# Fp32 gated attention mix: weights' loads and roundings, first keys, clearing, turned maxima, gate and last loads in other places

## The chip, the cores and the metric

The kernel runs on one core of a Trainium2 chip. The metric is device microseconds of one execution, as the median of several runs. Engines: PE is TensorE (matrix products), DVE is VectorE, ACT is ScalarE, POOL is GpSimd, SP is SyncE, which here issues nearly all DMAs. SP's queue is worked in order, so a DMA that waits for something holds up those behind it.

## The reference, cut to what matters

```python
# S=2048 tokens, D=448, H=16 heads of 28; x is A_x for both branches
g = sigmoid((x * gate_w).sum(-1, keepdims=True))
# A: each query sees 8 keys, at offsets 0, 2, ... 14 behind it
q, k, v = split_heads(x @ A_wqkv)
a = softmax(einsum("bhsd,bhswd->bhsw", q, k[idx]) * 28**-0.5, masked) @ v[idx]   # then merged @ A_wo
# B: full attention, 16 heads, 2048 x 2048 scores each
q, k, v = split_heads(x @ B_wqkv)
b = softmax(einsum("bhqd,bhkd->bhqk", q, k) * 28**-0.5) @ v                       # then merged @ B_wo
return g * a + (1 - g) * b
```

## The kernel before

Every fp32 product is computed as three products of rounded parts: an operand is split into a high part (`hi`, `xh`, `wh`: a ScalarE copy that rounds to fp32r) and a low part (`lo`, `xl`, `wl`: a subtraction, on VectorE or POOL), and high·high, high·low and low·high are summed in PSUM. Rounding a weight set thus costs ScalarE copies and POOL subtractions (`split_w`, in four pieces of its rows) once its load (`load_w`, tiles `raw` and, for the last 64 rows, `wt`) has landed.

The instructions of every engine run in the order in which the program writes them; no scheduler moves them. Order is therefore set by the loops and by small tables in the text.

**Projections.** A loop over 92 tiles `n`, in this order: tiles 0 to 11 (first queries and keys of B, weight set 0), 12 to 23 (set 1) and 24 to 27 (set 2), 512 tokens by 128 columns each; 28 to 43 values of B (set 3), 44 to 59, 60 to 75 and 76 to 91 the queries, keys and values of A (sets 4, 5, 6), each 128 tokens by 448 columns. From tile 10 on a tile is accumulated in two halves in two PSUM banks: ScalarE evacuates both (`raw`, L336 and L350), POOL adds them (L338, L351). For a q/k tile a step `finish` one tile later rounds (`qkh`, L341), and POOL subtracts (L342); both parts are stored to DRAM (`qk_hi`, `qk_lo`) and loaded again as keys (`KH`) and queries (`QP`). For A's tiles POOL adds into a staging tile `ast`, stored to `a_scr` every second tile. The last two columns of set 4 carry the gate (`zt`).

From tile 11 on TensorE works score products (L141, `s1`) into the projections, four per tile, of which VectorE takes maxima (`MX`, L158) for the softmax of B. When a group of 512 queries is through, `max_parts` splits its maxima, `max_turn` transposes them on VectorE (`nms`, L182) and `max_store` puts them in DRAM, the last two one tile later.

The table `loads` tells at which tile each weight set's load is written, `splits` at which two tiles its rounding is, two pieces per tile. After the exponential of the gate (n = 64) come a transposition of `1-g` on TensorE (n = 65), a copy `omT`, a store and sixteen loads `og`, then the first queries of the main stage (n = 66). SBUF tiles come from rings: the evacuations `raw` from a pool `pp` of eight (`pair`), weights and `ast` from a ring of three.

**Main stage.** 16 units (4 groups of heads by 4 blocks of 512 queries) of 16 key steps: step `st = 16u + kt` makes four score tiles on TensorE, two exponentials on ScalarE (`P`, L998) and the value products `av` of the step before (L957). Branch A (softmax over 8 taps) runs on POOL, VectorE and DMA beside it. `at(kind, st, f)` writes `f` into a step, at its start ("pre"), between the score tiles ("mid") or at its end. When A is done, `a_done(st)` loads the output weights and rounds one of seven blocks a step (`split_wo`). At a unit's end `fin_copy` copies its result out of PSUM (`osb`, L813) and an epilogue of seven more steps divides and stores it (`on_hi`, `on_lo`).

**Output products.** In the last 20 steps (from st = 236) TensorE also works the output projection for 16 tiles `j` of 128 rows. `op_queue(j)` lists its items: `op_mm` for seven blocks of rows (A's in `oah`, `oalo`, B's in `onhi`, `onlo`), `op_t` and `op_split` (transpose and split A's result of tile `j+1`, loaded into `oal` by `op_load_a`), `op_out`. `op_some(st, 7)` takes seven items a step; an item whose number in `READY` is above `st` stops the queue. `op_load_b(b, k)` loads B's results. After the last step come the leftovers, `op_rest` (the last head block of tiles 8 to 11), the last epilogue (`fin_t`, `fin_rec`, ...) and tiles 12 to 15.

Of the kernel before, what the change touches and what calls it, by code (L numbers as in the profile page):

```python
# [25 lines left out]
def gated_mix_kernel(ctx: ExitStack, tc: tile.TileContext, xT, xn, gw, wA, wB, woAB, out):  # L26
# [74 lines left out]
    def load_k(g, t, src):  # L101
        for h in range(4):
            r = D + 112 * g + DH * h
            dma_r(t[32 * h:32 * h + DH, :], src[r:r + DH, :])
# [85 lines left out]
    init_kh(KH[0])  # L190
# [6 lines left out]
    with tc.tile_pool(name="xp", bufs=1) as xp, tc.tile_pool(name="wp", bufs=2) as wp:  # L197
# [3 lines left out]
        def raw3():  # L201
            return wp.tile([128, 3, 450], F32, tag="raw", name="raw", bufs=3)
# [34 lines left out]
        def load_w(wi, tails=(False, True)):  # L237
            src, cols = WSRC[wi]
            if wi not in wraw:
                wraw[wi] = raw3(), ptile("wt"), sum(c1 - c0 for c0, c1 in cols) + 2 * (wi == GATE)  # L240
            r, t, _ = wraw[wi]
            for tail in tails:
                o = 0
                for c0, c1 in cols:
                    e = o + c1 - c0
                    if tail:
                        both(t[:, o:e], src[384:448, c0:c1])
                    else:
# [109 lines left out]
        def a_tile(n, i, j):  # L358
            k = j // 8
            if j % 2 == 0:  # L360
                stage[k] = wp.tile([128, 3, 450], F32, tag="raw", name="ast", bufs=3).rearrange(
                    "p a b -> p (a b)")[:, 0:896].rearrange("p (c j e) -> p c j e", c=8, j=2)
            add_halves(n, stage[k][:, :, j % 2, :], zt[:, j:j + 1] if tiles[n][0] == GATE else None)
            if j % 2 == 1:
                nc.sync.dma_start(a_own[i][:, :, j - 1:j + 1, :].rearrange("c p j e -> p c j e"), stage[k])
# [29 lines left out]
        nc.scalar.activation(zt, zt, AF.Exp)  # L395
        nc.scalar.activation(wh0[:, 0:3, wa], wr0, AF.Copy)
# [38 lines left out]
        firsts = [min(n for n, t in enumerate(tiles) if t[0] == wi) for wi in range(len(WSRC))]  # L435

        loads = {2: 17, 3: 22, **{wi: firsts[wi - 1] for wi in (4, 5, 6)}}
        splits = {1: firsts[1] - 4, 2: firsts[2] - 4, 3: firsts[3] - 4, **{wi: firsts[wi - 1] + 2 for wi in (4, 5, 6)}}
        for n, t in enumerate(tiles):
# [4 lines left out]
            for w in splits:  # L444
                if splits[w] <= n < splits[w] + 2:
                    split_w(w, (2 * (n - splits[w]), 2 * (n - splits[w]) + 1))
# [18 lines left out]
            if n == 4:  # L465
                for t in (*QP[0], *QP[1]):
                    nc.gpsimd.memset(t.bitcast(F32), 0.0)
            if n == 7:
                load_k(0, KH[0], qk_hi)
                load_qhi(0)  # L470
            if n == 8:
                for i in (1, 2):
                    nc.sync.dma_start(a_scr[i][:, 0:NJ, :].rearrange("c j e -> c (j e)").rearrange(
                        "c (a b) -> c a b", b=NJ), omg[0:8, None, :].to_broadcast([8, 56, NJ]))
            if n == 9:
                init_kh(KH[1])
                nc.gpsimd.memset(V[:, :, :, DH:], 1.0)
# [4 lines left out]
            if parts:  # L482
                u, t = parts.pop(0)
                max_store(u, max_turn(t))
            if finished and n < len(tiles) - 2:
                u = finished.pop(0)
                parts.append((u, max_parts(u)))
# [6 lines left out]
            if n == 65:  # L494
# [9 lines left out]
            if n == 66:  # L504
                load_q(0)
# [239 lines left out]
    def a_done(st):  # L745
        adone.append(st)
        load_wo()
        for k in range(7):
            at("pre", st + k + 1, lambda k=k: raw_wo(k))
            at("act", st + 6 + k, lambda k=k: split_wo(k))  # L750
# [174 lines left out]
    def op_queue(j):  # L925
# [7 lines left out]
            (0, lambda: op_split(j + 1)),  # L933
            (0, lambda: op_mm(j, bank, (2,))),
# [10 lines left out]
    READY[1, 3] = OP0 + 22  # L945
    for k in range(4):
        at("end", OP0 + 7 + k, lambda k=k: op_load_b(0, k))
        at("end", OP0 + 13 + k if k < 3 else OP0 + 18, lambda k=k: op_load_b(1, k))
# [56 lines left out]
    def op_some(st, n):  # L1005
        while n:
            if not opq:
# [4 lines left out]
                if j % 4 == 0 and 4 <= j:  # L1012
                    b = j // 4 + 1
                    for k in range(3):
                        op_load_b(b, k)
# [6 lines left out]
    for u in range(NU):  # L1022
        g, b = divmod(u, NB)
        for kt in range(NJ):
# [40 lines left out]
            if not OPS and s1c[0] == s1e:  # L1065
                s1_close()
                at("pre", st + 1, lambda: op_t(0))
                at("mid", st + 1, lambda: op_split(0))
# [10 lines left out]
    op_rest(9, accs[1])  # L1079
    fin_t(15)  # L1080
    fin_rec(15)
    op_rest(10, order[2])
    op_rest(11, order[3])
# [47 lines left out]
```

## Time and profile before

Three runs took 950.68, 952.6 and 953.49 us, median 952.6. The profiled execution took 950.85 us, its span is 949.1 us, and 1.75 us lie outside it. The mean granted clock of TensorE is 0.99.

| stage | us from the span's start | TensorE |
|---|---|---|
| projections, full tiles 0 to 9 | to about 34 | products |
| projections, half tiles with score products | about 34 to 277 | products, with the waits below |
| main stage without output products | 277 to 818 | two exponentials of about 1.0 us a step on ScalarE set the pace, 2.3 us |
| output products in the steps | 818 to 919 | 2.9 to 5.8 us a step |
| after the last `av` | 919 to 949 | products |

Rows read like this: start, duration, engine, line, instruction, result and operands; in brackets the idle time before it on its engine and what ended that. The pace of the projections is seen in evacuations two tiles apart, 5.81 us for q/k tiles and 5.25 us for A's:

```profile
70.19 1.03 ACT L336 ACTIVATE raw<-r 128x1024 f32<-128x1024 f32 x1 [1.48 <-PE r L284]
76.00 1.03 ACT L336 ACTIVATE raw<-r 128x1024 f32<-128x1024 f32 x1 [1.07 <-PE r L284]
...
224.49 0.92 ACT L350 ACTIVATE raw<-r 128x896 f32<-128x896 f32 x1 [1.62 <-PE r L289]
229.74 0.92 ACT L350 ACTIVATE raw<-r 128x896 f32<-128x896 f32 x1 [1.62 <-PE r L289]
```

### The profile page before, as it was taken

How to read it: one execution, taken by the hardware profiler on the slowest of the kernel's cores; microseconds unless marked ns; L12 is line 12 of the kernel's file. 1: busy time of each engine (PE TensorE's matmuls, PEld its weight loads, DVE VectorE, ACT ScalarE, POOL GpSimd, SP SyncE). 2: the span in 40 equal slices, each digit the busy share in tenths (PEclk: the TensorE clock that was granted, in tenths of full speed). 3: DMA queues.
4: the chain of work that ended last, by engine and by line, in shares of the span. 5: the costliest groups of instructions: out<-in, count | busy, mean ns of one | idle time of the engine just before them, and what ended most of it. 6: DMA issues, size and time to landing. Idle time of an engine off the chain costs nothing.

```text
span 949.1 us, 21412 instructions
## 1 busy us (share of the span) xinstructions
PE 921.4 (97%) x8398; PEld 548.4 (58%) x8398; DVE 735.9 (78%) x979; ACT 649.5 (68%) x798; POOL 621.4 (65%) x487
## 2 busy tenths in 40 slices
PE   8899899989999999999999999999999999999998
PEld 6798799979974444444444444444444443465657
DVE  6387699989978999999999999999998888400012
ACT  4355434333358888888888888888988889755541
POOL 2388746554448899999999999999993943100000
PEclk9999899999999999999999999999999999999999
DMA  9847403364437242333335331531412133344332
GB/s 277 249 169 218 151 1 89 84 162 117 111 106 225 71 130 55 84 98 89 91 89 127 108 92 45 133 97 25 106 42 52 32 77 105 112 143 128 108 111 87
DMA packets 101054, 104.36 MB, mean 110 GB/s; under 512 B 61676, under 2 KB 71292, under 8 KB 100056
## 3 DMA queue, kind: packets, MB, share of 16 engines
q1 hardware_dynamic: 100808, 102.72, 38.5%
q8 instruction: 66, 1.08, 0.5%
q10 hardware_dynamic: 144, 0.26, 0.1%
q14 instruction: 36, 0.29, 0.1%
HBM read 61.99 MB, written 40.48 MB: 108 GB/s over the span
## 4 chain that ended last, share of the span: by engine, by line
PE 87%; DMA 4%; POOL 3%; ACT 2%; SPq 2%; issue 2%; DVE 1%; ACTq 0%; POOLq 0%; DVEq 0%
PE T L995 29%; PE av L957 25%; PE r L289 13%; PE T L797 7%; PE r L284 4%; PE T L141 4%; PE r L141 3%; POOL qkh L342 1%; ACT P L998 1%; PE T L775 1%; POOL raw L338 1%; DMA wt<-in_wA 1%; DMA V<-in_xT 1%; SPq L98 1%; POOL wl L206 1%
## 5 line engine op out<-in xcount | busy, mean ns | idle before, releaser
L998 ACT ACTIVATE P<-T 128x1024 f32<-128x1024 f32 x512 | 497.2, 1024 | 96.6 <-PE T L995 95.9
L145 DVE TENSOR_REDUCE MX<-T 128x1 f32<-128x512 f32 x470 | 443.4, 954 | 42.0 <-PE T L141 17.2
L957 PE MATMUL av<-P,V 128*32 128x512 f32 x2048 | 272.7, 605 | 0.4 <-ACT osb L813 0.4
L995 PEld LDWEIGHTS T<-QH,KH 30*128 30x128 f32 x1024 | 91.2, 181 | 234.2 <-ACT P L998 203.2
L995 PE MATMUL T<-QH,KH 30*128 30x512 f32 x1024 | 221.3, 491 | 4.7 <-ACT P L998 3.3
L158 DVE TENSOR_REDUCE MX<-r 128x2 f32<-128x1024 f32 x160 | 192.2, 1221 | 38.2 <-PE r L141 37.1
L141 PE MATMUL T<-KH,QP 28*128 28x512 f32 x704 | 221.4, 460 | 0.0
L995 PE MATMUL T<-QH,KL 28*128 28x512 f32 x1024 | 189.2, 394 | 0.0
L995 PE MATMUL T<-QL,KH 28*128 28x512 f32 x1024 | 187.7, 393 | 0.0
L595 POOL TENSOR_TENSOR prod<-qt,kt 128x896 f32<-128x896 f32 x64 | 135.1, 2115 | 7.7 <-DMA kt<-a_scr 7.7
L350 ACT ACTIVATE raw<-r 128x896 f32<-128x896 f32 (+1 forms) x64 | 58.8, 919 | 99.4 <-PE r L289 95.6
L650 POOL TENSOR_TENSOR oat<-oat,prod 128x896 f32<-128x896 f32 x56 | 118.0, 2107 | 2.4
L141 PEld LDWEIGHTS T<-KH,QP 28*128 28x128 f32 x704 | 86.0, 181 | 23.2 <-ACT P L998 13.3
L645 POOL TENSOR_TENSOR prod<-vt,L 128x896 f32<-128x896 f32 x56 | 95.3, 1702 | 0.6
L141 PE MATMUL r<-KH,QP 64*128 64x512 f32 x320 | 90.6, 397 | 3.8 <-DMA QP<-qk_hi 2.6
L351 POOL TENSOR_TENSOR ast<-raw 128x448 f32<-128x448 f32 x48 | 55.1, 1151 | 59.1 <-ACT raw L350 37.2
L995 PEld LDWEIGHTS T<-QL,KH 28*128 28x128 f32 x1024 | 92.7, 184 | 0.0
L995 PEld LDWEIGHTS T<-QH,KL 28*128 28x128 f32 x1024 | 92.1, 183 | 1.0
L289 PE MATMUL r<-wh,xh 64*128 64x448 f32 (+1 forms) x512 | 84.7, 368 | 5.2 <-ACT raw L350 4.9
L957 PEld LDWEIGHTS av<-P,V 128*32 128x32 f32 x2048 | 40.3, 108 | 79.5 <-issue 73.8
L785 DVE TENSOR_TENSOR oalo<-T,oah 128x384 fp32r<-128x384 f32 x16 | 8.9, 557 | 88.3 <-ACT onhi L784 80.1
L289 PE MATMUL r<-wh,xl 64*128 64x448 f32 (+1 forms) x384 | 70.1, 366 | 0.0
(111 smaller groups left out, 1144.4 us busy)
## 6 DMA issues: line engine op xcount, KB each, us to landing
a_scr<-ast SPq DMA_DIRECT2D x24, 448.0 KB
qk_hi<-qkh SPq DMA_DIRECT2D x24, 256.0 KB
qk_lo<-qkh SPq DMA_DIRECT2D x24, 256.0 KB
rbc<-rs SPq DMA_DIRECT2D x60, 64.0 KB
KH<-qk_hi SPq DMA_DIRECT2D x16, 224.0 KB
QP<-qk_hi SPq DMA_DIRECT2D x64, 56.0 KB
KL<-qk_lo SPq DMA_DIRECT2D x16, 224.0 KB
QH<-qk_hi SPq DMA_DIRECT2D x64, 56.0 KB
```

The source lines that it names most:

```text
L141: nc.tensor.matmul(bank, qhis[u][h % 2][r, 128 * qs:128 * qs + 128], KH[u // NB % 3][r, 512 * kc:512 * kc + 512], start=True, stop=True)
L145: nc.vector.tensor_reduce(MX[:, n % NMX:n % NMX + k], bank, axis=X, op=ALU.max)
L158: nc.vector.tensor_reduce(m, PM[k], axis=X, op=ALU.max)
L289: nc.tensor.matmul(bank[:, 0:cols], x, ws[c][rows, k, 0:cols], start=first, stop=last)
L350: nc.scalar.activation(raw[:, :, 0:cols], PJ[n % 2][:, :, 0:cols], AF.Copy)
L595: nc.gpsimd.tensor_tensor(out=p, in0=qt[c], in1=kvt["k", c % 2][:, HALO - DIL * w:HALO - DIL * w + NJ, :], op=ALU.mult)
L645: nc.gpsimd.tensor_tensor(out=dst.rearrange("p j (h d) -> p j h d", d=DH), in0=kvt["v", c % 2][:, HALO - DIL * w:HALO - DIL * w + NJ, :].r ...
L650: nc.gpsimd.tensor_tensor(out=oat[c], in0=oat[c], in1=oat[c, w], op=ALU.add)
L797: writes(bank, nc.tensor.matmul(bank[:, :D], src, wo[c][:, k, :], start=(first and k == ks[0] and i == 0), stop=(last and k == ks[-1] and ...
L957: nc.tensor.matmul(av[32 * h:32 * h + 32, :], V[:, kt, 4 * g + h, :], tiles_[h], start=(kt == 0), stop=(kt == NJ - 1), skip_group_check=True)
L995: nc.tensor.matmul(bank[a], (KH[g % 3], KH[g % 3], KL[g % 2])[t][r, ks], (qh, ql, qh)[t][r, :], start=(t == 0), stop=(t == 2))
L998: nc.scalar.activation(p, RP[0] if a == "2" else mine, AF.Exp, scale=SCALE)
```

## The change

It gives other places to things that are done in any case; the mathematics is the same, and no product is added or removed. Line numbers of the changed kernel are up to five higher.

- First keys: the first queries are loaded at tile 3 (they were at 7), the first keys in two pieces, columns 0 to 1536 at tile 7 and the rest at tile 8.
- Weights: sets 2 to 6 are loaded at tiles 12, 16, 26, 40, 56 (before 17, 22, 28, 44, 60); set 3 is rounded at 24 and 25 as before, sets 4, 5 and 6 in four tiles each from 34, 48, 64 (before two tiles from 30, 46, 62). `wt` has a ring of its own, the weights' ring has two buffers, and `ast` comes from the ring of eight.
- Clearing: four `QP` buffers on ScalarE at the start (POOL at tile 4), `KH[1]` at the start (tile 9), ones into `V` at tile 32 (tile 9), the two small stores of zeros at 16 (8).
- Maxima are turned and stored three tiles after they are split (one before); gate transposition and first queries of the main stage at 68 and 69 (65 and 66).
- Last part: output weights' roundings three steps later (`d`; in this program `a_done` falls at 217, which gives 3), first `op_split` at the step's end, `op_load_b` as an item behind `op_split` for tiles 4 and 8, the last block of b = 1 loaded at OP0+16 and used from OP0+18 (OP0+18, OP0+22), `op_rest` in another order around the last epilogue's transposition.

```diff
-    init_kh(KH[0])
+    for t in KH:
+        init_kh(t)
...
-            return wp.tile([128, 3, 450], F32, tag="raw", name="raw", bufs=3)
+            return wp.tile([128, 3, 450], F32, tag="raw", name="raw", bufs=2)
...
-                wraw[wi] = raw3(), ptile("wt"), sum(c1 - c0 for c0, c1 in cols) + 2 * (wi == GATE)
+                wraw[wi] = raw3(), wp.tile([128, 450], F32, tag="wt", name="wt"), sum(c1 - c0 for c0, c1 in cols) + 2 * (wi == GATE)
...
-                stage[k] = wp.tile([128, 3, 450], F32, tag="raw", name="ast", bufs=3).rearrange(
-                    "p a b -> p (a b)")[:, 0:896].rearrange("p (c j e) -> p c j e", c=8, j=2)
+                stage[k] = pair("ast").rearrange("p a b -> p (a b)")[:, 0:896].rearrange("p (c j e) -> p c j e", c=8, j=2)
...
+        for t in (*QP[0], *QP[1]):
+            nc.scalar.activation(t, t0, AF.Copy)
         nc.scalar.activation(wh0[:, 0:3, wa], wr0, AF.Copy)
...
-        loads = {2: 17, 3: 22, **{wi: firsts[wi - 1] for wi in (4, 5, 6)}}
-        splits = {1: firsts[1] - 4, 2: firsts[2] - 4, 3: firsts[3] - 4, **{wi: firsts[wi - 1] + 2 for wi in (4, 5, 6)}}
+        loads = {2: 12, 3: 16, 4: 26, 5: 40, 6: 56}
+        splits = {1: (8, 2), 2: (20, 2), 3: (24, 2), 4: (34, 1), 5: (48, 1), 6: (64, 1)}
...
-            if n == 4:
-                for t in (*QP[0], *QP[1]):
-                    nc.gpsimd.memset(t.bitcast(F32), 0.0)
+            if n == 3:
+                load_qhi(0)
             if n == 7:
-                load_k(0, KH[0], qk_hi)
-                load_qhi(0)
+                load_k(0, KH[0], qk_hi, slice(0, 1536))
             if n == 8:
+                load_k(0, KH[0], qk_hi, slice(1536, S))
+            if n == 16:
                 for i in (1, 2):
                     nc.sync.dma_start(a_scr[i][:, 0:NJ, :].rearrange("c j e -> c (j e)").rearrange(
                        "c (a b) -> c a b", b=NJ), omg[0:8, None, :].to_broadcast([8, 56, NJ]))
-            if n == 9:
-                init_kh(KH[1])
+            if n == 32:
                 nc.gpsimd.memset(V[:, :, :, DH:], 1.0)
...
-            if parts:
-                u, t = parts.pop(0)
+            if parts and parts[0][0] <= n:
+                _, u, t = parts.pop(0)
                 max_store(u, max_turn(t))
-            if finished and n < len(tiles) - 2:
+            if finished and n < len(tiles) - 3:
                 u = finished.pop(0)
-                parts.append((u, max_parts(u)))
+                parts.append((n + 3, u, max_parts(u)))
...
-            if n == 65:
+            if n == 68:
                 b = PJ[(n + 1) % 2][:, 0, :]
                 nc.tensor.transpose(b[0:NJ, 0:128], omg, ident)
...
-            if n == 66:
+            if n == 69:
                 load_q(0)
...
+        d = -(st + 6) % NJ + 2 if (st + 6) % NJ > NJ - 7 else 0
         for k in range(7):
-            at("pre", st + k + 1, lambda k=k: raw_wo(k))
-            at("act", st + 6 + k, lambda k=k: split_wo(k))
+            at("pre", st + d + k + 1, lambda k=k: raw_wo(k))
+            at("act", st + d + 6 + k, lambda k=k: split_wo(k))
...
             (0, lambda: op_split(j + 1)),
+            (0, lambda: ([op_load_b(b + 1, k) for k in range(3)] if j in (4, 8) else None)),
             (0, lambda: op_mm(j, bank, (2,))),
...
-    READY[1, 3] = OP0 + 22
+    READY[1, 3] = OP0 + 18
...
-        at("end", OP0 + 13 + k if k < 3 else OP0 + 18, lambda k=k: op_load_b(1, k))
+        at("end", OP0 + 13 + k if k < 3 else OP0 + 16, lambda k=k: op_load_b(1, k))
...
-                if j % 4 == 0 and 4 <= j:
-                    b = j // 4 + 1
-                    for k in range(3):
-                        op_load_b(b, k)
...
-                at("mid", st + 1, lambda: op_split(0))
+                at("end", st + 1, lambda: op_split(0))
...
     op_rest(8, accs[0])
-    op_rest(9, accs[1])
     fin_t(15)
     fin_rec(15)
-    op_rest(10, order[2])
-    op_rest(11, order[3])
+    op_rest(9, order[2])
+    op_rest(10, order[3])
+    op_rest(11, accs[0])
```

SyncE around the first keys, before: tile 7's two stores, the whole keys, then the queries, then tile 8's stores.

```order
L98 DMA qk_hi<-qkh 128x512
L98 DMA qk_lo<-qkh 128x512
L98 DMA KH_151<-qk_hi 28x2048 x4
L98 DMA QP_155<-qk_hi 28x512
L98 DMA QP_156<-qk_hi 28x512
L98 DMA QP_155<-qk_hi 28x512
L98 DMA QP_156<-qk_hi 28x512
L98 DMA qk_hi<-qkh 128x512
L98 DMA qk_lo<-qkh 128x512
```

And now, from the first weights' last rows on (`wt`, written at tile 3):

```order
L212 DMA wt<-in_wB 64x64 x2
L98 DMA QP_155<-qk_hi 28x512
L98 DMA QP_156<-qk_hi 28x512
L98 DMA QP_155<-qk_hi 28x512
L98 DMA QP_156<-qk_hi 28x512
...
L98 DMA KH_151<-qk_hi 28x1536 x4
L98 DMA qk_hi<-qkh 128x512
L98 DMA qk_lo<-qkh 128x512
L98 DMA KH_151<-qk_hi 28x512 x4
```

The queries stand four tiles' stores earlier, and the keys' last quarter behind tile 8's stores.

ScalarE around the rounding of set 4 (`wh_1216<-raw` and `<-wt`), before, from the end of the q/k tiles into the values:

```order
L341 ACTIVATE qkh<-raw 128x512
L350 ACTIVATE raw<-r_132 128x2x448
L205 ACTIVATE wh_1216<-raw 128x450 x2
L350 ACTIVATE raw<-r_128 128x2x448
L205 ACTIVATE wh_1216<-raw 128x450
L205 ACTIVATE wh_1216<-wt 128x450
L350 ACTIVATE raw<-r_132 128x2x448
```

And now (`wh_1340`); the first piece stands five evacuations behind the last `qkh`:

```order
L351 ACTIVATE raw<-r_132 128x2x448
L206 ACTIVATE wh_1340<-raw 128x450
L351 ACTIVATE raw<-r_128 128x2x448
L206 ACTIVATE wh_1340<-raw 128x450
L351 ACTIVATE raw<-r_132 128x2x448
L206 ACTIVATE wh_1340<-raw 128x450
L351 ACTIVATE raw<-r_128 128x2x448
L206 ACTIVATE wh_1340<-wt 128x450
L351 ACTIVATE raw<-r_132 128x2x448
```

One piece now stands between two evacuations, four tiles later than before.

SyncE in the output products, tile 8, before: `op_load_b(3, 0)` to `(3, 2)` (six loads `onhi`, `onlo`) stand ahead of the loads of A's results.

```order
L807 DMA out<-res 128x448
L98 DMA onhi_11418<-on_hi 64x512
L98 DMA onlo_11419<-on_lo 64x512
L98 DMA onhi_11420<-on_hi 128x512
L98 DMA onlo_11421<-on_lo 128x512
L98 DMA onhi_11422<-on_hi 128x512
L98 DMA onlo_11423<-on_lo 128x512
L756 DMA oal<-oa_scr 128x448 x2
```

And now:

```order
L811 DMA out<-res 128x448
L760 DMA oal<-oa_scr 128x448
L98 DMA onhi_11418<-on_hi 64x512
L98 DMA onlo_11419<-on_lo 64x512
L98 DMA onhi_11420<-on_hi 128x512
L98 DMA onlo_11421<-on_lo 128x512
L98 DMA onhi_11422<-on_hi 128x512
L98 DMA onlo_11423<-on_lo 128x512
L760 DMA oal<-oa_scr 128x448
```

One `oal` load stands ahead of the six, the other behind.

More of the change, by code (lines that the diff above doesn't have):

```diff
@@ L98, in dma_r, with load_k @@
         nc.sync.dma_start(dst.bitcast(F32), src.bitcast(F32))
-    def load_k(g, t, src):
+    def load_k(g, t, src, c=slice(0, S)):
         for h in range(4):
             r = D + 112 * g + DH * h
-            dma_r(t[32 * h:32 * h + DH, :], src[r:r + DH, :])
+            dma_r(t[32 * h:32 * h + DH, c], src[r:r + DH, c])
     def load_part(u, name, src):
@@ L434, in gated_mix_kernel @@
         parts = []
-        firsts = [min(n for n, t in enumerate(tiles) if t[0] == wi) for wi in range(len(WSRC))]
-        loads = {2: 17, 3: 22, **{wi: firsts[wi - 1] for wi in (4, 5, 6)}}
-        splits = {1: firsts[1] - 4, 2: firsts[2] - 4, 3: firsts[3] - 4, **{wi: firsts[wi - 1] + 2 for wi in (4, 5, 6)}}
+        loads = {2: 12, 3: 16, 4: 26, 5: 40, 6: 56}
+        splits = {1: (8, 2), 2: (20, 2), 3: (24, 2), 4: (34, 1), 5: (48, 1), 6: (64, 1)}
         for n, t in enumerate(tiles):
@@ L444, in gated_mix_kernel @@
             for w in splits:
-                if splits[w] <= n < splits[w] + 2:
-                    split_w(w, (2 * (n - splits[w]), 2 * (n - splits[w]) + 1))
+                i, k = (n - splits[w][0]) * splits[w][1], splits[w][1]
+                if 0 <= i < 4:
+                    split_w(w, range(i, i + k))
             if n == 1:
```

## The prediction

> **What bounds the kernel now.** I read the page's first part, then TensorE's waits, then granted clock and timeline at each of those waits. The engine totals, and TensorE's waits by line (in total, times, longest):
>
> ```profile
> PE 921.4 (97%) x8398; PEld 548.4 (58%) x8398; DVE 735.9 (78%) x979; ACT 649.5 (68%) x798; POOL 621.4 (65%) x487
> PE r L289 <- ACT raw L350: 4.9, 2, 3.2
> PE T L995 <- ACT P L998: 3.3, 7, 1.0
> PE r L141 <- DMA QP<-qk_hi: 2.6, 1, 2.6
> PE r L284 <- ACT raw L336: 2.1, 1, 2.1
> PE r L496 <- DVE omg L493: 1.4, 1, 1.4
> PE T L775 <- DMA oal<-oa_scr: 1.3, 1, 1.3
> PE r L141 <- DVE MX L158: 1.3, 1, 1.3
> PE T L842 <- DVE res L920: 0.7, 1, 0.7
> PE r L289 <- ACT omT L498: 0.4, 1, 0.4
> ```
>
> TensorE is busy 97% of 949.1 us: in the projections and the tail nothing but its waits can be saved. The nine rows hold 18.0 us, and the change touches the cause of each. Three waits cost twice, since the granted clock falls behind them. Columns of the windows: stretch; length, then busy us (and instructions) of PE, PEld, DVE, ACT, POOL; clock, DMA share, GB/s.
>
> ```profile
> 42.00:44.00 2.00, 1.78 (x12) 1.73 (x14) 0.90 (x1) 0.00 (x0) 0.00 (x0) 0.80 0.74 187
> 44.00:46.00 2.00, 2.00 (x12) 2.00 (x10) 0.45 (x2) 0.00 (x0) 0.00 (x0) 0.50 0.79 252
> 46.00:48.00 2.00, 2.00 (x17) 2.00 (x16) 1.43 (x2) 1.03 (x2) 0.00 (x0) 0.85 0.36 78
> ...
> 90.00:92.00 2.00, 2.00 (x16) 1.64 (x14) 1.22 (x1) 2.00 (x5) 2.00 (x3) 0.74 1.04 262
> 92.00:94.00 2.00, 2.00 (x12) 1.52 (x12) 0.74 (x1) 0.49 (x1) 2.00 (x2) 0.50 0.86 238
> 94.00:96.00 2.00, 2.00 (x20) 1.61 (x18) 1.54 (x3) 1.03 (x1) 2.00 (x3) 0.91 0.94 305
> ...
> 112.00:114.00 2.00, 1.43 (x8) 1.25 (x10) 0.00 (x0) 2.00 (x4) 2.00 (x3) 0.50 0.44 170
> 114.00:116.00 2.00, 2.00 (x14) 1.78 (x12) 1.23 (x1) 0.26 (x1) 2.00 (x3) 0.50 0.00 0
> 116.00:118.00 2.00, 2.00 (x12) 1.73 (x12) 1.18 (x1) 0.07 (x1) 1.81 (x2) 0.50 0.00 0
> 118.00:120.00 2.00, 2.00 (x20) 1.81 (x20) 1.24 (x2) 0.85 (x1) 1.07 (x1) 0.93 0.00 0
> ```
>
> The work lost is the missing share of the clock times PE's busy time: 0.4+1.0+0.3 = 1.7 us behind the first wait, 0.5+1.0+0.2 = 1.7 behind the second, 0.7+1.0+1.0+0.1 = 2.8, call it 2.9 with the part of 110 to 112, behind the third. Waits of 2.1, 2.6 and 3.2 us end in half clock; at the 1.7 us wait (the 4.9 row less its longest) I saw none.
>
> **The change, part by part.**
>
> *First keys (tile 11).* SyncE's queue and the chain there:
>
> ```profile
> 29.71 2.42 DMA qk_hi<-qkh
> 34.37 1.63 SPq L98 DMA_DIRECT2D KH<-qk_hi  x4
> 36.05 1.67 SPq L98 DMA_DIRECT2D QP<-qk_hi  x4
> 36.05 6.04 DMA QP<-qk_hi
> ```
>
> The queries' load is issued at 36.05, behind the keys, and lands 6.04 us later, 2.6 us after TensorE asks at 39.65 (42.22 less the wait). In the new order the queries go at tile 3, some ten microseconds earlier, behind one more weight load and ahead of four stores. The keys come in two pieces. The first, three quarters, needs the store of 29.71, which landed at 32.13 (the whole needed tile 7's). In SyncE's order it still stands behind tile 7's stores, so it is issued at 34.4, give or take 0.8, and lands 2.4 us (that store) to 6.04 us (that load) later: 36.0 to 41.2, against 39.65. Wait left: 0 to 1.6. A quarter less data and no 1.67 us of query issue in between argue for the near half: I take 0.3 and no half clock. Gain 2.3+1.7 = 4.0; ends 1.0 (wait 1.6, clock still halved) and 4.3. SyncE issues four more loads for it (the keys' second piece, behind tile 8's stores, about 1.6 us by the keys' row); its queue waits for stores there, so nothing.
>
> *Third weights and turned maxima (tiles 22 to 28).*
>
> ```profile
> 87.65 1.04 ACT L205 ACTIVATE wh<-raw 128x448 fp32r<-128x448 f32 x2 [4.30 <-DMA raw<-in_wB]
> 88.30 2.24 POOL L206 TENSOR_TENSOR wl<-raw,wh 128x448 fp32r<-128x448 f32 x2 [2.83 <-ACT wh L205]
> 90.50 1.29 POOL L338 TENSOR_TENSOR raw<-raw 128x512 f32<-128x512 f32 x1
> 100.27 0.21 DVE L182 STREAM_TRANSPOSE nms<-nmt 128x32 f32<-128x32 f32 x1 [2.21 <-POOL nmt L177]
> ```
>
> ScalarE stands 4.30 us for weights requested two tiles before, with the evacuation that TensorE needs queued behind it. The load goes six tiles earlier, its three DMAs past the stores of six tiles on SyncE; the rounding stays. So 2.1 us of wait and 1.7 us of clock go. Then VectorE stands 2.21 us at a transposition that waits for POOL, TensorE loses 1.3 us behind the score maxima queued after it. The transposition moves two tiles later, 5 us and more, behind which POOL will have passed it: 1.3 goes too. Upper end 5.1. What is late next is POOL: it does two 1.29 us passes a tile, 2.58 us of the 2.9 that a tile lasts (the evacuations shown above), and four weight pieces of about 1.12 are 4.5 us on top. Before, the same backlog arose, but behind a TensorE that had stalled too. The 0.3 us a tile that POOL has free do not pay it off by tile 28. Evacuations have several buffers, so a few microseconds of POOL's lateness need not reach TensorE. Lower end: the whole 4.5 us comes out at TensorE, 5.1−4.5 = 0.6. I take 4.6, half a microsecond paid, nearer the upper end because ScalarE's own work fits.
>
> *Fourth weights and gate columns (tiles 26 to 37).*
>
> ```profile
> 110.67 1.04 ACT L205 ACTIVATE wh<-raw 128x450 fp32r<-128x450 f32 x2 [5.52 <-DMA raw<-in_gw]
> ```
>
> ScalarE waits 5.52 us; TensorE 3.2 (the longest of the first row), then 2.9 of clock. The load moves from 28 to 26, the roundings from 30 and 31 to one per tile at 34 to 37. Eight tiles lie between, 21 us at 2.62, against 5.52 for which ScalarE waited. One 0.57 us copy per tile (half of 1.04) fits ScalarE, which is idle half the time. Gain 6.1; lower end 3.2, were the half clock to come anyway.
>
> *Fifth and sixth weights.*
>
> ```profile
> 198.99 1.04 ACT L205 ACTIVATE wh<-raw 128x448 fp32r<-128x448 f32 x2 [3.98 <-DMA raw<-in_wA]
> ```
>
> The sixth's 1.7 us goes (load four tiles earlier, rounding two later). The fifth shows no wait of TensorE: nothing.
>
> *Gate.* Exponential at tile 64, transposition at 68 instead of 65: the wait for the gate (1.4) goes. TensorE still waits for the copy of the transposed gate, now behind one more evacuation of 0.92 us: 0.4 becomes about 1.3. Gain 0.5; ends 0 and 1.4.
>
> *Clearing.* Four query buffers go from POOL to ScalarE at the start. At 1.04 us for two passes that is 2.1 us, while the first weights are still being loaded. Nothing; 2.1 were that cover gone. The second key buffer's clearing joins POOL's first idle microseconds: nothing, by the same cover. The clearing in V (tile 9 to 32) and two small stores (8 to 16) lie where POOL and SyncE have room.
>
> *Tail.* ScalarE, TensorE:
>
> ```profile
> 794.92 0.62 ACT L813 ACTIVATE osb<-av 128x512 f32<-128x512 f32 x1
> 795.40 1.97 ACT L998 ACTIVATE P<-T 128x1024 f32<-128x1024 f32 x2
> 797.67 1.99 ACT L998 ACTIVATE P<-T 128x1024 f32<-128x1024 f32 x2
> ...
> 821.74 0.50 PE L995 MATMUL T<-QH,KH 30*128 30x512 f32 x2 [0.94 <-ACT P L998]
> ...
> 861.39 0.51 PE L995 MATMUL T<-QH,KH 30*128 30x512 f32 x4
> 862.31 1.06 PE L957 MATMUL av<-P,V 128*32 128x512 f32 x8
> 868.21 1.07 PE L957 MATMUL av<-P,V 128*32 128x512 f32 x8
> ```
>
> The output weights' rounding moves three steps on, clear of the copy `osb`. The step that ends at 795.40 held a rounding and the copy, which delayed the exponential by 0.48 (794.92 to 795.40); the next, with a rounding alone, took 2.27 and ran at TensorE's pace. Gain 0.4; ends 0 and 0.48. The split of the first transposed tile goes behind the step's exponentials: the 0.94 goes, 0.9. Between 862.31 and 868.21 two steps run without output work. Each needs 0.92 (861.39 to 862.31) plus 1.06 = 1.98 us of TensorE, and they take 5.90: lost 1.9. They are empty because an item waits for step 246. It now waits for 242, so every step has its seven items and none is left over: gain 1.9. The `oal` load of 1.3 us lateness now goes ahead of six large loads: 1.3. The last epilogue transposition comes one product later: 0.7 becomes about 0.1, 0.6. Tail 5.1; lower end 0, if TensorE waits as long for `load_b(2, 3)`, now at the end of the last step but used at once after the loop.
>
> *Sum.* 4.0+4.6+6.1+1.7+0.5+5.1 = 22.0. Profiled execution 950.85 (1.75 of it outside the span) − 22.0 = 928.85. The median of the runs shown, 952.6, lies 1.75 above the profiled execution; added, 930.6.
>
> The 6.3 us of clock in it (1.7+1.7+2.9) rest on reading the half clock as the waits' doing. What speaks for that: it follows each wait of 2.1 us or more, and no other row that I read. [...]
>
> **The rivals.**
>
> 1. *First keys still late.* The first piece lands at 41 or later: the DMA share is 0.93 in that stretch (the load of 36.05 needed 6 us). 2.3 to 2.8 us of the first term return, and the clock follows: about 934.
> 2. *POOL becomes the bound in tiles 24 to 30.* Price up to 4.0 of that term, with a wait of 2 us also the 1.7 of clock: 933 to 936. For it: POOL 2.00 of 2.00 in every window from 90 to 96. Against: TensorE at 2.00 there too.
> 3. *The tail gives nothing:* output steps limited by loads: 930.6+5.1 = 935.7. For it: the loads' chain held TensorE once (1.3), and the last step's load is new there. Against: SyncE's queue runs ahead of TensorE by several microseconds in the other steps.
> 4. *The half clock isn't due to the waits:* it falls at these places anyway, and 6.3 us stay: 936.9. Against: three drops, each right behind one of the three longest waits in the table.
> 5. *Slower: the staging ring.* The staging tile `ast` moves into the eight-buffer ring of the evacuations. Two tiles take two evacuations and one staging buffer, so an evacuation waits for the store made five tiles earlier.
>
> ```profile
> 213.07 8.09 SPq L502 DMA_DIRECT2D og<-og_scr  x16
> 221.26 0.38 SPq L365 DMA_DIRECT2D a_scr<-ast  x1
> 224.85 3.37 POOL L351 TENSOR_TENSOR ast<-raw 128x448 f32<-128x448 f32 x3 [5.95 <-DMA a_scr<-ast]
> ```
>
> A store lands 3.6 us after issue (221.26 to 224.85); five tiles at 2.62 are 13.1 us, and evacuation, addition and issue take 2 to 3 of them. It decides only if landing exceeds some 10 us; to lose 25 us (22 gained and 3 more) over some twelve turns of the ring, each has to wait 2.1 us, so 12 us of landing: 954. The sixteen gate loads, 8.09 us of SyncE's queue, stand ahead of the store of tile 71 in the new order and may use up this slack once, not twelve times.
> 6. *No effect:* the waits reappear at the next tile, because the weights' DMAs are limited by bandwidth (share 1.04 at 90 to 92): 951.
>
> **How the numbers follow.** Forecast 0.56 (927.5 to 933); rival 1, 0.10; 2, 0.12; 3, 0.09; 4, 0.04; 5, 0.03; 6, 0.02; better than all this, by clock that returns in places I did not count, 0.04 (926). The runs shown differ by 2.8 us, 0.3%, about what a measurement of this kernel can tell from no change. From 926.5 to 936.5 leaves out rival 5, 6, most of 4 and half of the better case: 0.11, and what I have not thought of. Faster 0.95, within 0.3% 0.02, slower 0.03.
>
> **What would show it.** First keys: the row `r<-KH,QP` with under 0.5 us of idle, clock 1.00 from 40 to 48. Weights: no row of `wh<-raw` with a DMA wait, clock 1.00 at 84 to 120. Gate: one wait of about 1.3 for `omT`, none for `omg`. Tail: no step under 3.5 us between two `av` rows after the output work begins, no wait for `oal`. I am wrong if TensorE shows new waits on POOL or on a DMA between tiles 24 and 30 or after the last `av`.

## The result and the profile after

The changed kernel takes 929.79 us (median of four runs, 928.69 to 930.45), the kernel before 952.11 in the same comparison: ratio 0.9765, interval 0.9747 to 0.9783. The forecast was 930.6 and a range of 926.5 to 936.5. A second comparison, the control below, gave 0.9783 (0.9746 to 0.9819). Ratios leave out slow executions, of which there was one, of 1630.54 us in the experiment `u_tail`.

The profiled execution took 928.69 us, its span is 926.9, 22.2 less than before. TensorE's total, and all its waits of over 0.5 us from the view of waits:

```profile
PE 914.1 (99%) x8398; PEld 545.6 (59%) x8398; DVE 733.3 (79%) x979; ACT 651.7 (70%) x802; POOL 620.8 (67%) x483
PE T L1000 <- ACT P L1003: 1.6, 3, 1.0
PE r L197 <- DVE omg L195: 1.5, 1, 1.5
PE r L285 <- DVE qkh L333: 1.4, 1, 1.4
PE T L1000 <- ACT raw L351: 1.0, 1, 1.0
PE r L290 <- ACT omT L500: 1.0, 1, 1.0
PE r L141 <- DVE MX L158: 0.7, 1, 0.7
PE r L141 <- DMA KH<-qk_hi: 0.5, 1, 0.5
```

Of the nine waits quoted in the prediction, those for weights, the turned maxima, `oal` and `res` are gone; the seven for `P` (3.3 in all) are now three (1.6); the one for first queries is now one of 0.5 for the keys; the two at the gate are now 1.0 and 0.7. Busy time fell as well, by 7.3 us, most of it because fewer products run at half clock: TensorE was busy for 15.9 us at half clock before and is for 3.4 now, and half of the difference, an estimate from the granted clock of 0.50 there, is 6.3 (a window of 2 us held 12 products at 44 to 46 us before, at 0.50, and 22 at 42 to 44 now, at 1.00). The windows that answer to those of before (clock is the third number from the right):

```profile
42.00:44.00 2.00, 2.00 (x22) 1.81 (x20) 1.84 (x2) 1.49 (x2) 0.38 (x1) 1.00 0.54 125
...
88.00:90.00 2.00, 2.00 (x22) 1.71 (x20) 1.75 (x3) 0.83 (x4) 2.00 (x2) 1.00 0.84 280
...
112.00:114.00 2.00, 2.00 (x22) 2.00 (x20) 2.00 (x2) 1.39 (x2) 1.70 (x3) 1.00 0.00 0
...
262.00:264.00 2.00, 2.00 (x21) 0.51 (x17) 1.53 (x2) 2.00 (x5) 0.99 (x10) 0.65 1.14 296
264.00:266.00 2.00, 2.00 (x20) 0.96 (x15) 0.65 (x2) 0.50 (x1) 0.00 (x0) 0.50 0.90 303
```

The three half-clock stretches of before are at 1.00. A new one stands at the entry of the main stage, at 262 to 266, which the prediction did not have. Before, the same place looked like this:

```profile
280.00:282.00 2.00, 2.00 (x26) 0.62 (x23) 1.65 (x2) 2.00 (x5) 1.01 (x10) 1.00 0.48 142
```

**Where the 22.2 us came from.** The timeline of both kernels, cut at marks that both have: the start of ScalarE's evacuation of tile n, the start of the value products `av` of the n-th step, and the end of the span. Each row is the length of a stretch.

| stretch | before | after | gain | predicted |
|---|---|---|---|---|
| start to evacuation 10 | 39.46 | 38.49 | 1.0 | 0 |
| evacuation 10 to 14 (first keys) | 16.10 | 12.62 | 3.5 | 4.0 |
| 14 to 23 | 26.24 | 26.23 | 0.0 | 0 |
| 23 to 36 (third and fourth weights, maxima) | 46.88 | 35.12 | 11.8 | 10.7 |
| 36 to 60 | 62.88 | 62.80 | 0.1 | 0 |
| 60 to 75 (sixth weights, gate) | 43.44 | 41.80 | 1.6 | 2.2 |
| 75 to 91 | 41.32 | 41.23 | 0.1 | 0 |
| evacuation 91 to `av` 10 (entry) | 27.48 | 29.06 | −1.6 | 0 |
| `av` 10 to 210 | 459.12 | 459.01 | 0.1 | 0 |
| `av` 210 to 224 (output weights) | 32.67 | 32.09 | 0.6 | 0.4 |
| `av` 224 to the end (tail) | 153.47 | 148.46 | 5.0 | 4.7 |
| span | 949.1 | 926.9 | 22.2 | 22.0 |

The sum is right to 0.2 us with two terms in it that weren't forecast, +1.0 at the start and −1.6 at the entry, and a few that were off. That these cancel so closely is luck. The experiments take them one by one. They are read by the same stretches, since the start alone varies: the evacuation of tile 10 began between 38.49 and 41.48 us in nine profiles of kernels that are the same up to there, and the medians of whole runs scatter accordingly.

Most of that scatter is a half clock too, one that I had not looked for. Before, at the start, behind a wait of 1.99 us for VectorE's copies of `x`, then in one of the nine, `u_tail`, behind 2.75 us for `qkh`; last, with the clock at 1.00, `i_all` behind 2.41 (from its view of waits):

```profile
8.86 1.12 PE L284 MATMUL r<-xh,wh 128*128 128x512 f32 x2 [1.99 <-DVE xh L399]
10.00:12.00 2.00, 2.00 (x6) 1.52 (x6) 1.97 (x4) 0.12 (x1) 0.00 (x0) 0.50 1.11 259
```

```profile
16.54 1.54 PE L285 MATMUL r<-xh,wh 128*128 128x512 f32 x4 [2.75 <-DVE qkh L333]
18.00:20.00 2.00, 2.00 (x6) 1.53 (x5) 0.00 (x0) 0.00 (x0) 0.00 (x0) 0.50 1.05 379
```

```profile
PE r L285 <- DVE qkh L333: 2.4, 1, 2.4
18.00:20.00 2.00, 2.00 (x10) 1.61 (x10) 0.19 (x1) 0.82 (x2) 0.00 (x0) 1.00 1.05 377
```

The four of the nine with half clock at the start (waits of 1.88 to 2.75 us there) reached tile 10 at 40.76 to 41.48, the five without (1.36 to 2.67) at 38.49 to 40.08. The control is the second run of the changed kernel, span 927.8, start without half clock.

### The profile page after: what moved, and what is told of

Same layout as the page of the kernel before. It is cut to its first block, busy times and chain, and to the rows that moved or that the text cites. A ratio compares the mean times of both kernels' runs of the same rounds, so it can differ in the third digit from the quotient of the medians.

```text
span 926.9 us, 21402 instructions
## 1 busy us (share of the span) xinstructions
PE 914.1 (99%) x8398; PEld 545.6 (59%) x8398; DVE 733.3 (79%) x979; ACT 651.7 (70%) x802; POOL 620.8 (67%) x483
## 4 chain that ended last, share of the span: by engine, by line
PE 92%; DMA 3%; ACT 2%; SPq 2%; DVE 1%; issue 1%; POOL 0%; ACTq 0%; DVEq 0%; POOLq 0%
PE T L1000 30%; PE av L962 26%; PE r L290 15%; PE T L801 8%; PE r L285 5%; PE r L141 4%; PE T L141 4%; DMA qk_hi<-qkh 1%; ACT P L1003 1%; SPq L98 1%; PE T L779 1%; DMA V<-in_xT 1%; DMA onlo<-on_lo 1%; DMA KH<-qk_hi 0%; DVE MX L145 0%
## 5 line engine op out<-in xcount | busy, mean ns | idle before, releaser
L141 PE MATMUL r<-KH,QP 64*128 64x512 f32 x320 | 94.2, 391 | 1.2 <-DVE MX L158 0.7
L290 PE MATMUL r<-wh,xh 64*128 64x448 f32 (+1 forms) x512 | 86.7, 363 | 1.0 <-ACT omT L500 1.0
```

Source lines behind the costliest of these rows:

```text
L141: nc.tensor.matmul(bank, qhis[u][h % 2][r, 128 * qs:128 * qs + 128], KH[u // NB % 3][r, 512 * kc:512 * kc + 512], start=True, stop=True)
L290: nc.tensor.matmul(bank[:, 0:cols], x, ws[c][rows, k, 0:cols], start=first, stop=last)
```

## The experiments

**First keys as before** (`u_keys`).

```diff
-            if n == 3:
-                load_qhi(0)
-            if n == 7: load_k(0, KH[0], qk_hi, slice(0, 1536))
-            if n == 8: load_k(0, KH[0], qk_hi, slice(1536, S))
+            if n == 7:
+                load_k(0, KH[0], qk_hi)
+                load_qhi(0)
```

> The changed kernel with the first keys as before (whole, then the queries, both at tile 7). Theory, waits plus the half clock behind them: TensorE waits 2.0 to 2.6 us for QP again, instead of 0.55 for KH, the granted clock falls to about 0.5 for 3 us behind it, and the kernel is 3.5 us slower than the changed one (929.8), 933.3. Rival, the clock fell there for another reason: the wait comes back and the clock stays at 1.00; 2 us slower, 931.8.

```profile
41.13 0.47 PE L141 MATMUL r<-KH,QP 64*128 64x512 f32 x1 [1.97 <-DMA QP<-qk_hi]
42.00:44.00 2.00, 2.00 (x15) 2.00 (x14) 1.23 (x1) 0.00 (x0) 0.00 (x0) 0.68 0.91 293
44.00:46.00 2.00, 2.00 (x12) 2.00 (x11) 1.23 (x1) 0.43 (x1) 0.00 (x0) 0.50 0.37 53
```

Ratio 0.9838 (0.9816 to 0.9859), median 933.0. The wait came back, and with it the half clock, while the rest of the changed kernel stayed as it is: the first theory holds in this profile. Evacuation 10 to 14 takes 15.53 us against 13.25 in the control and 12.62 in the first profile, so the loads' new place is worth 2.3 to 2.9, and 3.5, as the theory had it, only between the profiles of before and after, where the old wait was longer (2.56).

**Third weights loaded at 22** (`u_w3`).

```diff
-        loads = {2: 12, 3: 16, 4: 26, 5: 40, 6: 56}
+        loads = {2: 12, 3: 22, 4: 26, 5: 40, 6: 56}
```

> The changed kernel with the third weights loaded at tile 22 instead of 16. Theory: ScalarE waits about 4.3 us for in_wB at tile 24, TensorE 2.1 behind it, then half clock, 1.7 lost: 3.8 us slower, 933.6; the wait for MX does not return, since the transposition still stands two tiles later. Rival, POOL was the hidden bound: its four pieces now start 4 us later, with the q/k passes queued behind, and TensorE loses more than that, 5 to 6 us, 935 to 936.

```profile
85.27 1.04 ACT L206 ACTIVATE wh<-raw 128x448 fp32r<-128x448 f32 x2 [4.37 <-DMA raw<-in_wB]
87.28 1.22 PE L285 MATMUL r<-xh,wh 64*128 64x512 f32 x4 [2.18 <-ACT raw L337]
88.00:90.00 2.00, 2.00 (x12) 1.51 (x10) 1.00 (x1) 2.00 (x4) 2.00 (x3) 0.50 1.06 244
```

Ratio 0.9862 (0.9838 to 0.9886), median 935.05. Wait and half clock of before again; evacuation 23 to 36 takes 39.10 us against 35.12 in the control: 4.0, where the theory had 3.8. No wait for MX came back in this stretch, and none on POOL: the rival falls.

**Fourth weights loaded at 28, rounded at 30 and 31** (`u_w4`).

```diff
-        loads = {2: 12, 3: 16, 4: 26, 5: 40, 6: 56}
+        loads = {2: 12, 3: 16, 4: 28, 5: 40, 6: 56}
-        splits = {..., 4: (34, 1), ...}
+        splits = {..., 4: (30, 2), ...}
```

> The changed kernel with the fourth weights loaded at tile 28 and rounded at 30 and 31 as before. Theory: ScalarE waits 5 us for in_gw, TensorE about 3.2, then half clock for 5 us, 2.9 lost: 6.1 us slower, 935.9. Rival, load alone, no clock: 3.2 slower, 933.0.

```profile
102.56 1.05 ACT L206 ACTIVATE wh<-raw 128x450 fp32r<-128x450 f32 x2 [6.50 <-DMA raw<-in_gw]
104.47 1.12 PE L290 MATMUL r<-wh,xh 64*128 64x448 f32 x4 [4.83 <-ACT raw L351]
106.00:108.00 2.00, 2.00 (x14) 1.80 (x12) 1.23 (x1) 0.15 (x1) 2.00 (x3) 0.50 0.81 211
```

Ratio 0.9877 (0.9856 to 0.9898), median 936.46. The same stretch takes 43.01 us, 7.9 more than the control. The mechanism is the one expected, wait and half clock; the size is larger, since TensorE now waits 4.8 us and not 3.2. ScalarE stands 6.50 for the gate's columns, 5.52 before. Of the 1.6 us more, 1.2 is the load's: it ended ScalarE's wait 5.57 us after its issue (96.99 to 102.56), 4.37 before (106.30 to 110.67). The rest is that TensorE fell idle 2.6 us after that issue, and 3.1 before. Why the load took longer stays open.

**Maxima turned one tile after they are split** (`u_max`).

```diff
-                parts.append((n + 3, u, max_parts(u)))
+                parts.append((n + 1, u, max_parts(u)))
```

> The changed kernel with maxima turned one tile after they are split, as before. Theory: VectorE stands about 2 us at the transposition near tile 28, TensorE loses 1.3 us at MX: 931.1. Rival a, POOL's backlog is now longer there (it was 2.00 of 2.00 busy from 74 to 100 us in the changed kernel), VectorE stands 3 us or more: 2 to 3 us slower, 932 to 933. Rival b, with the weights earlier POOL has caught up by then: no change, 929.8.

```profile
95.94 0.21 DVE L182 STREAM_TRANSPOSE nms<-nmt 128x32 f32<-128x32 f32 x1 [3.53 <-POOL nmt L177]
97.31 0.50 PE L141 MATMUL r<-KH,QP 64*128 64x512 f32 x2 [2.62 <-DVE MX L158]
98.00:100.00 2.00, 2.00 (x16) 1.77 (x14) 1.52 (x2) 0.00 (x0) 2.00 (x3) 0.57 0.49 123
100.00:102.00 2.00, 2.00 (x15) 1.80 (x14) 1.23 (x1) 0.84 (x1) 0.70 (x1) 0.58 0.79 264
```

Ratio 0.9851 (0.9824 to 0.9877), median 934.84. The stretch takes 39.56 us, 4.4 more than the control. That is rival a, and more than it: VectorE stands 3.53 us, TensorE waits 2.62 and not 1.3, and now the clock halves behind it, which the kernel before did not do there. With the weights earlier TensorE no longer stands at tile 24, POOL gets no pause in which to catch up (it is at 2.00 of 2.00 in the changed kernel from 74 to 100 us; before, it had a pause of 2.83 us that ended at 88.30, as the prediction shows), and whoever waits for POOL waits longer. So the early transposition cost 1.3 us of TensorE's waiting in the kernel before and costs 4.4 with the earlier weights; the two later tiles are what makes POOL's backlog harmless. The three parts undone one at a time cost 4.0+7.9+4.4 = 16.3, together they brought 11.8: they are not additive.

**Control, entry of the main stage** (`r_after`, `i_entry`, `i_fill2`). The half clock at 262 to 266 stands behind two waits of 1.0 us, 2.2 us apart, which the kernel before had too.

> The changed kernel once more, as the control of this group on its chip. Every theory: the same ratio to the kernel before as at first, 0.9765, waits as in the first profile, and half clock at the entry of the main stage again if two waits of 1.0 us within 2.2 us are enough for it.

```diff
             if n == 69:
                 load_q(0)
+        for _ in range(4):        # i_fill2: range(2)
+            nc.tensor.matmul(PM[1][:, 1, :], xh[1][:, 0, 0:128], xh[0][:, 0, :], start=True, stop=True)
```

> The changed kernel with four products more, of no use to the result, on TensorE behind the last projection tile, into a bank that nobody reads. They lie in the 1.0 us in which TensorE waits for the last evacuation. Theory, the clock falls when too much idle time falls into one stretch of about 3 us, in one piece or two: with half of the idle filled the clock stays at 1.00 at the entry, 1.5 to 2 us faster than the control. Rival, the clock falls at the entry for another reason (DMA load, a change of PSUM use): clock as in the control, time the same or 0.1 slower.

> As the kernel with four products at the entry, with two: of the two waits of 1.0 us there some 0.55 and 1.0 are left. Theory, idle time of under 1.7 us within one stretch leaves the clock at 1.00, as the single waits up to 1.68 did: no half clock at the entry. Rival, the entry is near the edge, and the clock halves with 1.5 us of idle in 3 too.

The windows behind the second wait, of the control, then of the kernels with four and with two products:

```profile
263.00:265.00 2.00, 2.00 (x17) 0.80 (x18) 1.31 (x2) 1.56 (x5) 0.93 (x10) 0.50 1.01 282
265.00:267.00 2.00, 2.00 (x20) 0.70 (x15) 0.83 (x2) 0.88 (x1) 0.00 (x0) 0.71 0.97 350
```

```profile
263.00:265.00 2.00, 1.52 (x19) 0.94 (x23) 1.59 (x4) 2.00 (x5) 1.79 (x10) 1.00 0.95 249
265.00:267.00 2.00, 2.00 (x23) 0.83 (x15) 1.81 (x2) 1.58 (x3) 0.00 (x0) 1.00 0.95 323
```

```profile
264.00:266.00 2.00, 1.75 (x19) 0.94 (x23) 1.61 (x4) 2.00 (x5) 1.76 (x10) 1.00 0.93 249
266.00:268.00 2.00, 2.00 (x27) 0.88 (x22) 1.76 (x3) 1.59 (x3) 0.00 (x0) 1.00 1.00 335
```

The control halves again, the filled ones stay at 1.00. Evacuation 91 to `av` 10 takes 28.97 us in the control, 27.74 with four products, 27.53 with two, and 27.48 in the kernel before: the half clock costs 1.2 to 1.5 us here, a little less than the theory's 1.5 to 2. In whole runs this doesn't show: ratios 0.9783 (0.9746 to 0.9819), 0.9789 (0.9754 to 0.9823) and, in another group, 0.9784 (0.9761 to 0.9808). The two waits unfilled stand in ten profiles of this study, and the clock halved in eight of them, within 2 to 4 us of the first wait's end; in the kernel before and in `u_tail` (below) it did not. The same two waits can thus halve the clock or not; the last section shows what tells most of these cases apart. None of the three filled ones halved it (the third is `i_all`, next).

**The entry filled and three small waits taken away** (`i_all`).

```diff
-            if n == 7: load_k(0, KH[0], qk_hi, slice(0, 1536))
+            if n == 5: load_k(0, KH[0], qk_hi, slice(0, 1024))
+            if n == 7: load_k(0, KH[0], qk_hi, slice(1024, 1536))
...
             if n == 64:
+                ez = [sp.tile([128, NJ], F32, name="ez") for _ in range(2)]
+                for sgn, e in zip((-1.0, 1.0), ez):
+                    nc.scalar.activation(e, zt, AF.Exp, scale=sgn)
+            if n in (65, 66):     # sum and reciprocal of g_t at 65, of omg at 66, on VectorE
+                ...
...
+            if n == 68:           # transposition, copy omT, store, loads og: now ahead of
+                ...               # a_tile(68), whose evacuation is next on ScalarE
...
+        for _ in range(4):        # the four products of i_entry
+            ...
```

> The changed kernel with the four products at the entry, the first keys' first piece cut to 1024 columns and issued at tile 5 (the third quarter at 7, the last at 8), the gate's sums and reciprocals on VectorE one and two tiles after their exponentials, and the gate's transposition copied ahead of tile 68's evacuation. Theory: no wait for KH (0.5), none for MX at tile 65 (0.7), half of the wait for omT (0.5), no half clock at the entry (1.7): 3.4 us faster than the control. Rival, these waits are covered by what comes after them, ScalarE's pace in the main stage: nothing but the start of the main stage comes earlier, and the gain is under 1 us.

```profile
PE r L290 <- ACT omT L462: 0.4, 1, 0.4
```

Median 924.78 (924.5 to 925.4) against the control's 929.19 on the same chip, 4.4 us less, where the theory had 3.4; ratio to the kernel before 0.9733 (0.9699 to 0.9767). No wait of TensorE for KH or MX is left in its view of waits, and the one for `omT` is the row above. By stretches the gain over the control is 1.7 at the first keys (13.25 to 11.59), 1.5 from evacuation 64 to 75 (31.32 to 29.81) and 1.4 at the entry (28.97 to 27.59). It is the fastest kernel of the study; waits of under a microsecond were worth at least their own length.

**Query buffers cleared on POOL** (`u_clear`).

```diff
-        for t in (*QP[0], *QP[1]):
-            nc.scalar.activation(t, t0, AF.Copy)
...
+            if n == 2:
+                for t in (*QP[0], *QP[1]):
+                    nc.gpsimd.memset(t.bitcast(F32), 0.0)
```

> The changed kernel with the four query buffers cleared on POOL again, right behind its first rounding, at 6.5 to 8.5 us. Theory, VectorE's rounding copies of x stand while POOL clears: the pair of copies that took 0.76 us takes 2.2 as before the change, TensorE's second wait at the start grows from 0.4 to about 2.0 us, and the first evacuated half tile is 0.5 to 1.5 us later. Rival, the 2.2 us was a late load of x: the pair stays at 0.76, the time is the same.

POOL's clearing and VectorE's pair of copies here, then the pair in the changed kernel:

```profile
6.53 1.92 POOL L468 MEMSET QP<- 128x512 f32 x4
6.74 2.32 DVE L399 CAST xh<-V 128x512 fp32r<-128x512 f32 x2 [1.66 <-DMA V<-in_xT]
```

```profile
6.47 0.76 DVE L401 CAST xh<-V 128x512 fp32r<-128x512 f32 x2 [1.39 <-DMA V<-in_xT]
```

The copies stand while POOL clears, as the theory has it: the pair takes 2.32 us instead of 0.76. But the time does not follow: ratio 0.9784 (0.9747 to 0.9822), evacuation 10 at 39.38, between the ones of the nine without half clock. TensorE's wait for the copies is 1.4 us, the later one for `qkh` 0.9 where the changed kernel has 1.4. What the clearing on POOL did before, a wait of 1.99 and half clock behind it, it did not do here, where the wait was shorter. So part of the 1.0 us at the start may be the clearing's; this run does not show it, and it stays open.

**Gate at 65 and 66** (`u_gate`).

```diff
-            if n == 68:
+            if n == 65:
                 b = PJ[(n + 1) % 2][:, 0, :]
...
-            if n == 69:
+            if n == 66:
                 load_q(0)
```

> The changed kernel with the gate's transposition at tile 65 and the first queries at 66, as before. Theory, the gate's move is worth next to nothing, since its waits only change names (1.4 for omg and 0.4 for omT before, 0.7 for MX and 1.0 for omT now): from tile 64 to tile 75 the same time as the control (31.3 us) or up to 1.4 us more, if the wait for omg comes on top of that for MX. Rival, the late transposition made the wait for MX: it goes when undone.

TensorE's waits near the gate, first with the gate at 65, then in the control:

```profile
191.89 0.68 PE L290 MATMUL r<-wh,xh 64*128 64x448 f32 x4 [0.77 <-ACT omT L500]
```

```profile
190.38 0.51 PE L141 MATMUL r<-KH,QP 64*128 64x512 f32 x2 [0.68 <-DVE MX L158]
199.33 0.67 PE L290 MATMUL r<-wh,xh 64*128 64x448 f32 x3 [0.96 <-ACT omT L500]
```

Evacuation 64 to 75 takes 30.40 us, 0.9 less than in the control (31.32). In the kernel with the other parts changed, moving the gate back is a gain, and the rival came true: the wait for MX goes. One wait at 65 takes the place of two; as I read it, VectorE's delay by the gate's sums passes while TensorE waits for the copy anyway. In whole runs it is not clear of noise (0.9775, 0.9751 to 0.9798).

**The whole last part as before** (`u_tail`): `op_load_b`, `READY`, the place of `op_split(0)`, the order of `op_rest` and `d = 0`, all lines of the diff from `a_done` on.

> The changed kernel with everything from the output weights' rounding on as before (its steps, the place of the first split, the loads ahead of tiles 4 and 8, the numbers in READY, the order after the last step). Theory: the tail's terms are there alone and add up, two steps without output work come back, a wait for oal of 1.3 us, one of 0.9 behind P and one of 0.7 behind res: 5.1 us slower from step 224 to the end than the changed kernel. Rival, output steps give back elsewhere what one place gains: under 3 us.

```profile
806.32 0.50 PE L999 MATMUL T<-QH,KH 30*128 30x512 f32 x2 [0.94 <-ACT P L1002]
...
888.10 0.63 PE L779 MATMUL T<-ident,oal 128*128 128x128 f32 x4 [1.39 <-DMA oal<-oa_scr]
909.04 0.66 PE L846 MATMUL T<-ident,osb 128*128 128x128 f32 x4 [0.72 <-DVE res L924]
```

Ratio 0.9836 (0.981 to 0.9862). The waits are those of the kernel before within 0.05 us, and from `av` 224 to the end it takes 153.69 us against 148.45 in the control: 5.2, with 0.45 more in the stretch ahead (32.55 against 32.10) for the output weights. The theory had 5.1. The two steps without output work are back too: from `av` 243 to 245 it takes 5.9 us, as in the kernel before, and 10.1 with output work in the changed one.

## Why the prediction was right, point by point

- *First keys:* right in kind, 0.5 to 1.2 high. The wait left was 0.55 us (0.8 in the control), where I took 0.3 out of 0 to 1.6. The first piece's load landed 4.42 us after its issue at 35.14, between my two ends, as the chain of the profiled execution has it:

```profile
30.24 3.62 DMA qk_hi<-qkh
35.14 4.42 DMA KH<-qk_hi
```

  The store ahead of it took 3.62 us and not 2.42.
- *Weights and maxima, 10.7 forecast, 11.8 measured.* The steps are right: waits of ScalarE for weights became waits and half clock of TensorE, and all of these went. The split into terms was off: `u_w4` puts 7.9 and `u_max` 4.4 where I had 6.1 and 1.3. I read each term from the kernel before, but its size depends on which other stalls are left: the maxima's was small there because an earlier stall had given POOL time. The forecast of 0.5 lost to POOL didn't come true: no wait of TensorE stands between 84 and 116 us. Rival 2 stayed away because of the very step that I priced at 1.3.
- *Sixth weights and gate, 2.2 forecast, 1.6 measured.* The sixth weights brought 1.9 of it (tile 60 to 64, 12.42 to 10.47), and the gate's term is the one that failed in sign: tile 64 to 75 takes 31.32 where it took 31.02. I counted the wait for `omg` as gone, and missed that VectorE's four small instructions would then delay the score maxima (0.7). `u_gate` shows that its move costs 0.9 beside the other parts.
- *Clearing:* nothing forecast, nothing measured by itself; but its cost before was there to be read, in VectorE's copies of 2.22 us and the wait of 1.99 with half clock behind it, and I only looked for it on ScalarE and POOL.
- *Tail, 5.1 with the output weights, 5.6 measured;* `u_tail` confirms it alone. No step is under 3.5 us once the output work has begun. Of the waits two of 0.2 and 0.4 us are left at 802 to 804; `load_b(2, 3)` held nobody.
- *Half clock.* Rival 4 is out: in the three stretches the clock fell only where a wait was put back (`u_keys`, `u_w3`, `u_w4`). But the reading behind it, that a wait of 2.1 us or more halves the clock and nothing else does, was wrong on both sides. The kernel before had a fourth drop, at the start behind 1.99 us, and none at its entry, with the same two waits; the changed one has the drop at the entry, 1.6 us. By the trace's clock record of the kernel before, the half clock lasts 3.41 us behind the first two waits of the prediction and 6.83 behind the third.
- *Rivals 5 and 6.* The staging ring held nobody: tiles 36 to 60 and 75 to 91 take 0.1 us less each. The times of both rivals, 954 and 951, were counted from the profiled execution and not from the median as the forecast was; from the median they would be 955.6 and 952.6.

## What to carry to other kernels

Price a stall by what its stage loses, clock included, and ask of each stall that goes who had used it to catch up: the waits behind it grow, and a part that looks small (a transposition two tiles later) can be what keeps the others' gain. A total can be right while its terms are not, so compare by stretches between marks that both kernels have; where the start varies by 3 us, this tells 1 us apart and the medians do not. A short wait of an engine that is busy nearly all the time, here TensorE at 99%, was worth at least its full length: in `i_all` the stretch of the first keys gave 1.7 us for a wait of 0.8.

## What the runs showed of the hardware

- **In these profiles, whether a wait halved the clock went by where it fell on a grid of 3.413 us, and not by its length alone.** Of the single waits from the first tile's products to tile 91 in the thirteen profiles, none of up to 1.68 us halved the clock, of sixteen from 1.88 to 4.83 us twelve did, and the four that did not were 1.88, 2.10, 2.41 and 2.67. Two waits of 1.0 us within 3.2 us, at the entry of the main stage, did in eight of ten profiles, and in none of three in which one of the two was filled or cut to 0.34. The traces show what most of this turned on. In all thirteen the granted clock changes only at whole multiples of 3.413 us from the first entry of its record (in `u_gate` at 7.13, 17.37, 20.79, 263.13 and 266.55 us). Idle time can be summed by these slots: of the 20 drops from full clock up to the last 6 us of the span, 18 follow a slot with 1.67 us or more of TensorE's idle time, and no other slot at full clock there, of 3460, has more than 1.59. The four waits that left the clock alone each lie across the border of two slots. Here is the same wait of 1.88 us in `u_gate`, within one slot, and then in `u_w4`, across a border (a slot's idle time is 3.41 less the first busy time):

```profile
13.96:17.37 3.41, 1.53 (x8) 1.29 (x8) 3.08 (x8) 1.69 (x6) 0.00 (x0) 1.00 1.08 255
17.37:20.79 3.42, 3.42 (x10) 2.65 (x9) 0.52 (x1) 1.15 (x3) 0.00 (x0) 0.50 1.04 383
```

```profile
11.33:14.74 3.41, 2.60 (x12) 1.75 (x10) 2.47 (x5) 3.08 (x8) 0.00 (x0) 1.00 1.12 327
14.74:18.15 3.41, 2.35 (x10) 1.97 (x11) 2.29 (x7) 0.87 (x3) 0.00 (x0) 1.00 1.06 252
18.15:21.57 3.42, 3.42 (x16) 2.77 (x16) 2.31 (x4) 2.94 (x6) 0.00 (x0) 1.00 1.05 392
```

  The two drops that this does not explain stand at the entry, in the first profile of the changed kernel and in `u_w4`, behind slots with 1.09 and 1.27 us of idle time; they stay open. The grid is read from the traces; no run was made to place a wait on it. About half a slot of idle time went ahead of 18 of the drops, and the shortest single wait that halved the clock was 1.88 us (`u_gate`).
- **VectorE's copies stood while POOL cleared.** A pair of 128x512 copies from SBUF to SBUF took 0.76 us with no memset beside it (the changed kernel), and 2.22 (the kernel before) and 2.32 (`u_clear`) beside four memsets of 0.48 us each. No run shows why. The maxima on VectorE, which read PSUM, showed no such loss beside POOL's additions and subtractions in the projections: each took 1.16 to 1.23 us in the kernel before, with a median of 1.22 both for the 36 that lie wholly beside POOL's work and for the 13 that lie beside none.
